# Unit 0 of a local-attention and channel-mix kernel split in two units of whole words, with a new plan

## The chip, the cores and the metric

The kernel runs on one core of one Trainium2 chip. The metric is device time in microseconds of one execution; the kernel before takes 609.59 (median of 3 runs, 609.19 to 614.19). The engines are PE (TensorE: matmuls into PSUM; PEld are its weight loads), DVE (VectorE), ACT (ScalarE), POOL (GpSimd) and SP (SyncE, which here only issues DMAs).

## What is computed

Attention with a window of 64 over 8 batches, 8 heads, 576 positions and 64 columns per head; its output is the input x of a channel mix with a gate (512 model columns, 1024 hidden columns). Cut from the reference:

```python
scores = np.where((rel >= 0) & (rel < 64), scale * np.matmul(q, k.transpose(0, 1, 3, 2)), -1e9)
scores = scores - np.max(scores, axis=-1, keepdims=True)
attn = np.exp(scores)
attn = attn / (np.sum(attn, axis=-1, keepdims=True) + 1e-09)
x = np.matmul(attn, v)                       # heads side by side: 512 columns
...
xk = mu_k * x + (1.0 - mu_k) * x_prev        # x_prev: x moved by one position
xr = mu_r * x + (1.0 - mu_r) * x_prev
k = np.maximum(xk @ w_k, 0.0)
v = k * k @ w_v
r = 1.0 / (1.0 + np.exp(-(xr @ w_r)))
return (r * v).astype(np.float32)
```

q, k, v and the mu are 32-bit; w_k (512x1024), w_v (1024x512) and w_r (512x512) come as 64-bit floats and are made into 32-bit ones on the chip.

## The kernel before

**Attention.** Positions go in blocks of 64, two blocks (128 tokens) are a group, 36 groups in all. A group's tiles by the names in the profile: scores s on PE from k and q; DVE folds the two key blocks into one (`s<-own,s`, `s<-s,hide`), takes the maximum (`most`); ACT makes exponentials and their sums (`pr`, in a "lean" group one row of heads at a time with the sum taken along; in the others DVE subtracts and sums); DVE scales (`rs`, `pr<-pr,rs`); for the first ten groups PE transposes (t), later ones go through DVE and two DMAs; DVE masks (`pt`, two steps); PE multiplies with v (x), and ACT copies x into the unit's buffer `xu`.

**Channel mix.** Tokens go in units of 256 (18 of them, `UNITS`). Each unit has mixing (xk and xr), k products (`m<-xk,w`, then relu `kf` and square `ks`), r products (`m<-xr,w`, then `th`, `r` and the gate's share `r<-th,r`), v products (`m<-ks,w`), and the gated result (`r<-m,r`), which SP stores. A product is made for two column blocks of 128 at a time into one PSUM bank.

**Weights.** Twenty chunks of 128x512 (four of w_r, eight of w_k, eight of w_v). Each is loaded by a DMA, then decoded from 64 to 32 bits: one ACT step (`wt<-w`), two short DVE steps on `wt`, and two long ones (`wt<-w,wt` and, last, `w<-w,wt`, which puts the 32-bit word in place). From unit 1 on, products don't use the word but two parts of it, a high and a low one in a one-pass type (fp32r), three one-pass records per product. The parts are made by `split`: ACT copies the high part (CAST `w<-w`), DVE subtracts for the low one (`w<-w,w`); for chunk 0 (`PE_LOW`) PE makes the low part with two matmuls of 512 columns (`m<-w,ident`, `m<-w,minus`) and ACT copies it. The decoded words must stay until their chunk is split.

**Unit 0** uses the whole words, before they are split: mixing on PE with diagonal matrices (`mixer`, made on ACT), then r, k and v products of 256 columns as whole-word matmuls. Each of these is two records in the trace. It needs x of groups 0 and 1, and each product its decoded chunk. Unit 1 mixes with ACT and DVE (`e<-xu,mu` on ACT, blend `e<-xu,muk,e` and `e<-xu,mur,e` on DVE, then high and low parts xk, xr), later units with DVE alone for the blend.

**What sets the order.** Every step is a Piece with an engine, a key, an assumed cost and what it needs and holds. `play()` walks a clock of its own over all pieces, on each engine takes the ready one with the lowest key, and the instructions are emitted in that order; each engine then runs them strictly in it. The keys of the plan are the tables at the top: `BEGIN` (attention bursts), `DECODE` and `SPLIT` (chunks), `MIX_*`, `SOFT`, `MIXER`, the set `LEAN`, and `ORDER` for the first loads on SP's queue. All instructions carry one line number in the profile, since a wrapper records them.

## Time and profile before

| | us |
|---|---|
| median of 3 runs | 609.59 (609.19 to 614.19) |
| profiled execution, its own time | 611.41 |
| its span, first to last instruction | 609.5 |

Busy time of each engine over the span, from the page's first part (share, and count of instructions):

```profile
PE 585.8 (96%) x7131; PEld 572.5 (94%) x7131; DVE 437.8 (72%) x974; ACT 334.2 (55%) x741; POOL 9.4 (2%) x39
```

The second part cuts the span in 40 slices of 15.2 us; a digit is the busy share in tenths:

```profile
PE   2689999999999999999999999999999999999997
DVE  5889999486959586868686778768777668686321
```

PE is full from the fourth slice to the last but one; DVE is full only in slices four to six. What differs from slice to slice lies in the first five.

### The profile page before, as it was taken

What the parts mean: (1) busy time and instruction counts of PE and PEld (TensorE: products, weight loads), DVE (VectorE), ACT (ScalarE), POOL (GpSimd) and SP (SyncE); (2) the same over time, 40 slices, a digit from 0 to 9 for tenths busy, and PEclk for the clock granted to TensorE, in tenths of its full rate; (3) what the DMA queues carried; (4) which work ended last, traced back from release to release, by engine and by line L of the source; (5) the groups of instructions that cost most, each with busy time, mean ns of one, the idle gap of its engine ahead of it and who ended that gap; (6) DMA issues with size and microseconds to landing.
All of it is one profiled execution on the core that took longest, in us unless ns stands there. A gap on an engine that the chain in (4) does not pass through costs nothing.

```text
span 609.5 us, 17060 instructions
## 1 busy us (share of the span) xinstructions
PE 585.8 (96%) x7131; PEld 572.5 (94%) x7131; DVE 437.8 (72%) x974; ACT 334.2 (55%) x741; POOL 9.4 (2%) x39
## 2 busy tenths in 40 slices
PE   2689999999999999999999999999999999999997
PEld 1578899999999999999999999999999999999997
DVE  5889999486959586868686778768777668686321
ACT  5758878381927182727363646354645455454442
POOL 5000000000000000000000000000000000000000
PEclk9999999999999999999999999999999999999999
DMA  9877232314433242425242525242524252121011
GB/s 276 282 238 250 62 97 61 99 51 122 131 93 117 74 146 79 139 74 163 80 130 70 157 71 148 70 140 88 143 84 139 75 153 72 55 70 36 2 35 36
DMA packets 98269, 67.18 MB, mean 110 GB/s; under 512 B 15504, under 2 KB 92304, under 8 KB 98192
## 3 DMA queue, kind: packets, MB, share of 16 engines
q1 hardware_dynamic: 97904, 66.09, 35.9%
q8 instruction: 56, 0.92, 0.6%
q14 instruction: 21, 0.17, 0.1%
q10 hardware_dynamic: 288, 0.00, 0.0%
HBM read 49.81 MB, written 16.25 MB: 108 GB/s over the span
## 4 chain that ended last, share of the span: by engine, by line
PE 89%; DMA 6%; DVE 2%; ACT 1%; SPq 1%; issue 0%; ACTq 0%
PE m L94 79%; PE s L94 5%; PE x L94 5%; DMA w<-w_k 2%; DMA w<-w_r 1%; DMA w<-w_v 1%; DVE wt L94 1%; SPq L94 1%; DMA k<-kT 1%; PE t L94 1%; DVE w L94 0%; ACT pr L94 0%; ACT e L94 0%; DVE r L94 0%; ACT xu L94 0%
## 5 line engine op out<-in xcount | busy, mean ns | idle before, releaser
L94 PE MATMUL m<-xk,w 128*128 128x256 f32 x1696 | 225.1, 282 | 0.3 <-issue 0.3
L94 PE MATMUL m<-ks,w 128*128 128x256 f32 x1696 | 222.6, 281 | 0.8 <-issue 0.5
L94 PEld LDWEIGHTS m<-xk,w 128*128 128x128 f32 x1696 | 208.2, 188 | 2.7 <-issue 0.4
L94 PEld LDWEIGHTS m<-ks,w 128*128 128x128 f32 x1696 | 207.4, 188 | 3.3 <-issue 1.1
L94 PE MATMUL m<-xr,w 128*128 128x256 f32 x848 | 122.6, 280 | 0.0
L94 PEld LDWEIGHTS m<-xr,w 128*128 128x128 f32 x848 | 108.9, 188 | 0.8 <-ACT xr L94 0.2
L94 ACT ACTIVATE kf<-m 128x512 f32<-128x512 f32 x72 | 42.9, 597 | 88.7 <-PE m L94 87.7
L94 DVE TENSOR_TENSOR ks<-kf,ks 128x512 fp32r<-128x512 f32 x68 | 46.0, 678 | 57.6 <-ACT ks L94 57.5
L94 ACT COPY xu<-x 128x512 f32<-128x512 f32 (+3 forms) x28 | 19.4, 712 | 119.0 <-PE x L94 118.9
L94 DVE SCALAR_TENSOR_TENSOR r<-m,r 128x512 f32<-128x512 f32 (+1 forms) x37 | 24.9, 676 | 65.8 <-PE m L94 65.8
L94 PE MATMUL s<-k,q 64*64 64x128 f32 (+1 forms) x1152 | 37.5, 279 | 9.5 <-DMA q<-qT 9.5
L94 PEld LDWEIGHTS s<-k,q 64*64 64x64 f32 x1152 | 31.9, 140 | 13.1 <-issue 7.8
L94 ACT ACTIVATE kf<-kf 128x512 f32<-128x512 f32 x68 | 43.3, 636 | 1.6
L94 ACT CAST ks<-kf 128x512 fp32r<-128x512 f32 x68 | 42.5, 625 | 1.5
L94 PE MATMUL x<-pt,v 64*64 64x64 f32 (+1 forms) x1664 | 35.9, 237 | 0.1
L94 PEld LDWEIGHTS x<-pt,v 64*64 64x64 f32 x1664 | 34.7, 136 | 1.0 <-issue 0.8
L94 DVE TENSOR_TENSOR pt<-pr,sides 128x512 f32<-128x512 f32 x52 | 34.1, 684 | 0.7 <-DMA pr<-far 0.7
L94 DVE COPY_PREDICATED s<-own,s 128x256 f32<-128x256 uint32 (+1 forms) x72 | 25.5, 395 | 11.6 <-PE s L94 10.7
L94 DVE SCALAR_TENSOR_TENSOR r<-th,r 128x512 f32<-128x512 f32 x36 | 24.6, 682 | 11.6 <-ACT r L94 11.5
L94 DVE SCALAR_TENSOR_TENSOR e<-d,mur,xu 128x256 f32<-128x256 f32 (+3 forms) x88 | 31.1, 405 | 0.0
L94 DVE SCALAR_TENSOR_TENSOR e<-d,muk,xu 128x256 f32<-128x256 f32 (+3 forms) x88 | 30.6, 403 | 0.0
L94 ACT ACTIVATE th<-m 128x512 f32<-128x512 f32 x36 | 21.7, 603 | 13.7 <-PE m L94 13.6
(65 smaller groups left out, 517.4 us busy)
## 6 DMA issues: line engine op xcount, KB each, us to landing
k<-kT SPq DMA_DIRECT2D x28, 384.0 KB, 4.7
q<-qT SPq DMA_DIRECT2D x32, 256.0 KB, 4.1
v<-v SPq DMA_DIRECT2D x128, 64.0 KB, 3.3
far<-tr SPq DMA_DIRECT2D x26, 256.0 KB, 2.0
pr<-far SPq DMA_DIRECT2D x104, 64.0 KB, 1.9
outT<-r SPq DMA_DIRECT2D x23, 256.0 KB, 2.2
w<-w_k SPq DMA_DIRECT2D x8, 512.0 KB, 6.1
w<-w_v SPq DMA_DIRECT2D x8, 512.0 KB, 6.3
```

The costliest lines, as they stand in the source:

```text
L94: return lambda *args, **kw: tc.keep_in_program_order(op(*args, **kw))
```

## The change

`UNITS` becomes (2, 2) and then 17 units of 4: the first 256 tokens are two units of 128, each made of one group, and both use whole words (`EXACT = 2`). Unit 2 takes the place of unit 1 in how it mixes. The products of both are put in with keys from a table: r and k of unit 0, r and k of unit 1, and only then v of both. The results ks of two pairs of column blocks share one buffer, there are four r buffers for three. All the plan's tables are new; `PE_LOW` is empty, so DVE makes every low part; `LEAN` loses groups 6 and 11.

```diff
-UNITS = (4,) * 18
+UNITS = (2, 2) + (4,) * 17
-R_BUFS = 3
+R_BUFS = 4
...
-LEAN = {0, 1, 2, 3, 4, 6, 7, 8, 10, 11}
-PE_LOW = {0}
+LEAN = {0, 1, 2, 3, 4, 7, 8, 10}
+PE_LOW = set()
+EXACT = 2
+FRONT = (("r", 0, 0), ("k", 0, 8), ("r", 1, 24), ("k", 1, 32), ("v", 0, 48), ("v", 1, 64))
...
-ORDER = (*"w k0 q0 w k1 q1 w k2 w v1 w w w v0 q2 v3 w w q5 w w v4 w k3 w k4 w k5 q3 v2 w v5 w w w w w".split(),
-         *"q4".split())
+ORDER = (*"q0 k0 w k1 q1 w w k2 w v0 w q4 q2 v1 w w w v3 w v2 q3 w w w k5 v4 w w w k3 v5 w q5 w w w".split(),
+         *"k4 w".split())
...
-        if u == 0:
+        if u < EXACT:
             (_, _, _, x0), = parts(u)
...
-            state, scratch, result = [], Hold("tmp"), Hold("ks")
+            state, scratch = [], Hold("tmp")
+            result = k2[-1][1] if first and i % 2 else Hold("ks")
...
-                    state.append(act.tile([P, 2, n], F32, name="ks0", tag="ks", bufs=KS_BUFS))
+                    if i % 2 == 0:
+                        both.append(act.tile([P, 2, 2, n], F32, name="ks0", tag="ks", bufs=KS_BUFS))
+                    state.append(both[-1][:, i % 2])
...
+        early[u] = xk, xr, gate, k2
+        if u < EXACT - 1:
+            continue
+        for what, e, key in FRONT:
+            xk, xr, gate, k2 = early[e]
+            if what == "r":
+                r_units(key, *xr, gate, n, True)
+            elif what == "k":
+                k_units(key, *xk, k2, n, True)
+            else:
+                v_units(key, e, k2, gate, n, True)
```

What moves is shown at three places, before and after. In these rows a name's number stays where it tells tiles apart.

PE, start of the program, before: scores of group 2, values of group 1 (the four x rows), then mixing of unit 0 (three of its four pieces) and the first r product.

```order
L94 MATMUL s<-k,q 64x128 x16
L94 MATMUL x<-pt,v 64x128 x4
L94 MATMUL x<-pt,v 64x64 x8
L94 MATMUL x<-pt,v 64x128 x4
L94 MATMUL x<-pt,v 64x64 x8
L94 MATMUL m<-xu,mixer 128x256 x12
L94 MATMUL t<-ident,pr 128x4x32 x4
L94 MATMUL m<-xr_448,w_118 128x256
```

The same place after; the transposition t in the first row is group 1's, and group 0's values stand ahead of it:

```order
L96 MATMUL t<-ident,pr 128x4x32 x4
L96 MATMUL s<-k,q 64x128 x16
L96 MATMUL m<-xu,mixer 128x128 x8
L96 MATMUL x<-pt,v 64x128 x4
L96 MATMUL x<-pt,v 64x64 x8
L96 MATMUL x<-pt,v 64x128 x4
L96 MATMUL x<-pt,v 64x64 x8
L96 MATMUL m<-xu,mixer 128x128 x8
L96 MATMUL m<-xr_437,w_126 128x128
```

Mixing of unit 0 begins ahead of group 1's values instead of behind them.

PE, v products of unit 0 before: the rows from the low part for chunk 0 to the first product of the second pair of columns (`ks_683,w_474` is its first chunk). w_538 is the chunk that DVE decodes last.

```order
L94 MATMUL m<-w_118,ident 128x512
L94 MATMUL m<-w_705,minus 128x512
L94 MATMUL m<-ks_687,w_516 128x256
L94 MATMUL m<-ks_687,w_531 128x256
L94 MATMUL m<-ks_720,w_538 128x256 x2
L94 MATMUL m<-ks_720,w_543 128x256 x2
L94 MATMUL m<-ks_842,w_556 128x256 x2
L94 MATMUL m<-ks_842,w_605 128x256
L94 MATMUL t<-ident,pr 128x4x32 x4
L94 MATMUL m<-ks_683,w_474 128x256
```

After: `ks_604` and `ks_684` are unit 0's, `ks_803` and `ks_830` unit 1's, w_525 is the first chunk of w_v, and w_610 the one that DVE decodes last.

```order
L96 MATMUL m<-ks_830,w_590 128x128
L96 MATMUL m<-ks_830,w_599 128x128
L96 MATMUL m<-ks_684,w_610 128x128 x2
L96 MATMUL m<-ks_604,w_525 128x128 x2
L96 MATMUL m<-ks_604,w_557 128x128 x2
L96 MATMUL m<-ks_604,w_564 128x128 x2
L96 MATMUL m<-ks_604,w_577 128x128 x2
L96 MATMUL m<-ks_684,w_583 128x128 x2
L96 MATMUL m<-ks_684,w_590 128x128 x2
L96 MATMUL m<-ks_684,w_599 128x128 x2
L96 MATMUL m<-ks_684,w_610 128x128 x2
L96 MATMUL m<-ks_830,w_610 128x128 x2
```

The chunk decoded last now closes the first pair of columns of unit 0, and the second pairs of both units stand behind it; before, the fifth chunk of the first pair was the one decoded last, and 24 products stood from it on.

DVE, the end of decoding before (group 4's first steps, unit 1's blends e, the last step of w_538):

```order
L94 SCALAR_TENSOR_TENSOR w_543<-w_543,wt 128x512
L94 TENSOR_REDUCE most<-s 128x4 x2
L94 TENSOR_TENSOR w_709<-w_128,w_709 128x512
L94 SCALAR_TENSOR_TENSOR wt<-w_538,wt 128x512
L94 SCALAR_TENSOR_TENSOR e<-xu,muk,e 128x256 x2
L94 SCALAR_TENSOR_TENSOR w_538<-w_538,wt 128x512
L94 SCALAR_TENSOR_TENSOR e<-xu,muk,e 128x256 x2
```

And after (unit 2's blends, the last step of w_610):

```order
L96 TENSOR_TENSOR s<-s,hide 128x2x64
L96 SCALAR_TENSOR_TENSOR wt<-w_610,wt 128x512
L96 TENSOR_REDUCE most<-s 128x4 x2
L96 SCALAR_TENSOR_TENSOR e<-xu,muk,e 128x256 x4
L96 SCALAR_TENSOR_TENSOR e<-xu,mur,e 128x256 x4
L96 SCALAR_TENSOR_TENSOR w_610<-w_610,wt 128x512
L96 TENSOR_TENSOR w_824<-w_126,w_824 128x512
```

All eight blends stand ahead of the last decode step instead of two, and the first split of a chunk behind it. On SP's queue q and k of group 0 now lead, and the chunks of w_k are issued ahead of the v that crosses two batches (eight DMAs).

More of the change, by code (lines that the diff above doesn't have):

```diff
@@ L43 @@
 USTEPS = 40
[L44 to L57 removed]
+BEGIN = (-219.0, -153.0, -33.5, -13.0, 19.5, 25.0, 56.5, 67.0, 99.5, 120.5, 130.5, 154.5, 211.5, 216.5, 218.5,
+    231.5, 264.5, 268.5, 276.0, 329.0, 337.5, 341.0, 393.0, 415.0, 446.5, 455.0, 466.0, 513.5, 526.5, 546.5,
+    551.0, 563.0, 602.0, 609.0, 620.0, 627.0, 695.0)
+DECODE = (318.0, -62.5, -227.0, 24.0, 94.5, -374.5, -288.0, 11.0, 5.0, -70.0, 202.0, 362.5, -58.0, 381.0,
+    -84.5, 120.0, -310.0, -167.0, 12.5, 192.5)
+MIX_0 = (-210.5, -67.0, -379.5, 166.0)
+MIX_1 = (154.0, -358.5)
+MIX_N = (365.0, 83.5)
+SPLIT = (313.75, 318.25, 49.5, 394.5, -175.25, 79.5, 239.5, 145.75, -311.0, -373.0, 196.5, 173.5, 122.5,
+    -255.5, 153.5, 86.0, 227.0, 426.5, 233.0, 101.0)
+SOFT = (-196.5, -253.0, -250.0, 61.5, 287.0, 357.5)
+LEAN = {0, 1, 2, 3, 4, 7, 8, 10}
+PE_LOW = set()
+EXACT = 2
+FRONT = (("r", 0, 0), ("k", 0, 8), ("r", 1, 24), ("k", 1, 32), ("v", 0, 48), ("v", 1, 64))
+MIXER = (64.5, 212.5)
 SPARE = {512: 2}
@@ L658, in mix @@
         pk = None
-        if u >= 2:
+        if u > EXACT:
             scratch = Hold("tmp")
@@ L684, in blend @@
             def blend(e=e, mu=mu, xs=xs, hold=hold):
-                if u >= 2:
+                if u > EXACT:
                     e.append(pair(tmp.tile([P, 512], F32, name="e", tag="tmp", bufs=TB), n))
@@ L701, in low @@
                 dve.tensor_sub(xs[0][:, 1, cs, :n], e[0], xs[0][:, 0, cs, :n].bitcast(F32))
-            if u >= 2:
+            if u > EXACT:
                 p = Piece("DVE", key, 2 * over(n) + 130, blend, [pk], [own_], [held["x", u], scratch], port=True)
@@ L778, in k_units @@
     def k_units(key, xk, hold, made, k2, n, first):
+        both = []
         for i in range(NF // 2):
@@ L803, in k_units @@
             p = Piece("ACT", key, acts(2 * n), relu, [p], [scratch], [bank])
-            p = Piece("ACT", key, acts(2 * n) + 20, square, [p], [result] if first else [], [scratch])
+            p = Piece("ACT", key, acts(2 * n) + 20, square, [p], [result] if first and i % 2 == 0 else [],
+                      [scratch] + ([result] if first and i % 2 else []))
             if first:
@@ L877, in attn_rwkv_kernel @@
             prefetch(t, [("q", g + 2), ("k", g + 2)] + [("v", g)] * (t > LATE))
+    early = {}
     for u, nb in enumerate(UNITS):
@@ L883, in attn_rwkv_kernel @@
         xk, xr = ([], Hold("xk"), []), ([], Hold("xr"), [])
-        if u == 0:
-            keys = MIX_0
-        elif u == 1:
+        if u < EXACT:
+            keys = MIX_0[2 * u:2 * u + 2]
+        elif u == EXACT:
             keys = MIX_1
@@ L891, in attn_rwkv_kernel @@
             mix(u, i, keys[i], xk, xr)
-        if u == 0:
-            r_units(base, *xr, gate, n, True)
-            k_units(base + 8, *xk, k2, n, True)
-        else:
+        if u >= EXACT:
             k_units(base, *xk, k2, n, False)
             r_units(base + 16, *xr, gate, n, False)
-        v_units(base + 24, u, k2, gate, n, u == 0)
-        if u == 0:
-            for i in range(len(chunks)):
-                split(i)
+            v_units(base + 24, u, k2, gate, n, False)
+            continue
+        early[u] = xk, xr, gate, k2
+        if u < EXACT - 1:
+            continue
+        for what, e, key in FRONT:
[6 more added lines that the diff above has]
+                v_units(key, e, k2, gate, n, True)
+        for i in range(len(chunks)):
+            split(i)
     for p in play():
```

16 lines of the change are left out of this document (2 added, 14 removed).

## The prediction

> **What bounds the kernel now.** I read the page's totals first, then the engines by stage, then the chain that ended last, and only then single rows of the start.
>
> ```profile
> span 609.5 us, 17060 instructions
> 0.00:27.04 27.04, 10.21 (x185) 8.29 (x185) 18.96 (x44) 17.70 (x65) 8.67 (x32) 1.00 0.88 270
> 27.04:34.55 7.51, 5.91 (x28) 4.94 (x29) 5.31 (x13) 5.64 (x24) 0.00 (x0) 1.00 0.65 221
> 34.55:68.03 33.48, 32.07 (x289) 27.48 (x287) 32.26 (x72) 24.06 (x69) 0.10 (x1) 1.00 0.74 237
> 68.03:81.30 13.27, 13.06 (x133) 11.38 (x133) 12.89 (x26) 10.43 (x25) 0.00 (x0) 1.00 0.06 20
> 81.30:606.34 525.04, 524.58 (x6500) 520.43 (x6500) 367.97 (x824) 276.37 (x563) 0.63 (x6) 1.00 0.32 95
> 606.34:609.50 3.16, 0.00 (x0) 0.00 (x0) 0.42 (x1) 0.00 (x0) 0.00 (x0) 0.90 0.37 124
> ```
>
> After the stretch and its length the columns are busy time of PE, PE's weight loads, DVE, ACT and POOL, then granted clock, DMA share and GB/s. From 81.30, where the first product of split words starts, to 606.34, PE idles 0.46 us of 525.04; the tail is 3.16 us. The products of split words and the attention groups behind that point are the same after the change. So the time is the moment of that first split product (I call it the anchor, 81.30 now) plus 528.2, and whatever the change gives must show as an earlier anchor. Ahead of it PE idles 20 us, 18.4 of them before 34.55, while DVE is 96% busy from 34.55 to 68.03. Here is what leads to the anchor, from the chain of waits:
>
> ```profile
> 70.21 1.57 PE m L94 x6
> 71.78 0.44 PE t L94 x4
> 72.22 7.35 PE m L94 x34
> 79.57 1.03 PE s L94 x32
> 80.60 0.70 PE x L94 x48
> 81.30 8.04 PE m L94 x69
> ```
>
> And the rows at about 62 to 68 us (engine, operation, tile written <- tiles read):
>
> ```profile
> 61.80 0.63 PE L94 MATMUL x<-pt,v 64*64 64x128 f32 x24
> 66.56 0.87 DVE L94 SCALAR_TENSOR_TENSOR e<-xu,muk,e 128x256 f32<-128x256 f32 x2
> 67.35 0.68 DVE L94 SCALAR_TENSOR_TENSOR w<-w,wt 128x512 uint32<-128x512 uint32 x1
> 68.13 1.97 PE L94 MATMUL m<-ks,w 128*128 128x256 f32 x8 [0.48 <-issue]
> ```
>
> The row at 67.35 is the last decode step of the last weight chunk (w_538); it ends at 68.03, and PE, which had come to exactly that chunk in its order, starts 0.1 us later. From there to the anchor PE does 24 whole-word products (48 records: 8, 6 and 34), one transposition and one group's scores and values, 13.3 us without a real gap. So the anchor is the end of decoding on DVE, T = 68.03, plus 13.3. The idle PE of the first 27 us is not by itself on this path: DVE is.
>
> **The change part by part.** First the price of a whole-word record of 128 columns, which the trace does not have. A record of 256 columns costs 7.35 / 34 = 0.216 us. Streaming half the columns would be 0.108. The other bound comes from rows with 128x128 weights loaded for each record:
>
> ```profile
> 34.09 0.63 PE L94 MATMUL t<-ident,pr 128*128 128x128 f32 x4 [1.60 <-ACT xr L94]
> 34.55 0.60 PE L94 MATMUL m<-xr,w 128*128 128x256 f32 x2
> L94 PEld LDWEIGHTS m<-xr,w 128*128 128x128 f32 x848 | 108.9, 188 | 0.8 <-ACT xr L94 0.2
> ```
>
> Four transposing records of 128 columns go from 34.09 to 34.55, 0.115 each, and the one-pass records from 81.30 take 8.04 / 69 = 0.117, each with its own load. So 0.108 to 0.117; I take 0.115, the row with the same column count. Twice as many records at 0.115 make 0.230 per pair instead of 0.216: the 192 whole-word records of unit 0 (mixing, r, k, v) cost 41.5, the 384 after it 44.2, 2.7 us more PE work. All but the part behind T lies in PE time that waits for DVE anyway.
>
> A rule speaks against this. The Trainium skill, "TensorE: Matmul & The Clock Gate", LDWEIGHTS, gives a load about 1/1.2 ns per column, an estimate of 107 ns for 128 columns, and in The mechanism says that a load overlaps a running matmul only when the row group differs. By its first part load and stream would be equal at 128 columns and the sum stays; by the second nothing would hide, which is the third rival below. The trace does not agree with the second: 0.115 to 0.117 per record with a 128x128 load in each leaves no room for both in turn.
>
> Start of PE. These are the rows that lead to the first mixing:
>
> ```profile
> 6.81 1.55 PE L94 MATMUL s<-k,q 64*64 64x64 f32 x32 [6.81 <-DMA q<-qT]
> 8.46 0.30 DVE L94 TENSOR_TENSOR s<-s,hide 128x128 f32<-128x128 f32 x1 [0.71 <-PE s L94]
> 9.63 0.39 ACT L94 ACTIVATE mixer<-ident,mur 128x128 f32<-128x128 f32 x1
> ...
> 11.97 0.20 ACT L94 ACTIVATE most<-most 128x8 f32<-128x8 f32 x1
> 16.02 1.09 PE L94 MATMUL t<-ident,pr 128*128 128x128 f32 x4 [2.98 <-DVE pr L94]
> 21.37 1.56 PE L94 MATMUL x<-pt,v 64*64 64x128 f32 x32
> 27.04 5.45 PE L94 MATMUL m<-xu,mixer 128*128 128x256 f32 x24 [0.97 <-ACT xu L94]
> ```
>
> Group 0's q and k are now issued ahead of the first weight chunk, which moves its scores from 6.81 to about 5.4; ACT no longer makes eight mixers (9.63 to 11.97, 2.3) ahead of its exponentials, so these begin at about 9.4; its values need not follow group 1's transposition, and unit 0 needs only this group. Its transposition comes at about 13.4 and its values at 16.5; ACT then still makes group 1's exponentials and the mixers before it copies x, so the first mixing moves from 27.04 to about 21. The r products wait for group 2's exponentials on ACT too, and move from 34.55 to about 28.4, 6.2 us earlier. None of it counts unless T moves.
>
> T. DVE's waits until then, with the row kinds that change:
>
> ```profile
> DVE wt L94 <- ACT wt L94: 8.2, 3, 5.4
> DVE s L94 <- PE s L94: 1.1, 2, 0.7
> DVE rs L94 <- ACT rs L94: 1.0, 2, 0.5
> DVE pt L94 <- PE x L94: 0.6, 1, 0.6
> L94 DVE SCALAR_TENSOR_TENSOR r<-m,r 128x256 f32<-128x256 f32 x2 | 0.8, 425 | 2.6 <-PE m L94 2.6
> L94 DVE SCALAR_TENSOR_TENSOR r<-th,r 128x512 f32<-128x512 f32 x2 | 1.4, 690 | 0.0
> ```
>
> The waits add to 10.9 (5.4 of them at the start), so DVE works 57.1 us up to T. After the change the order has the same 20 decodes and the same four and a half groups ahead of the last decode step (now of w_610), but all eight blends e of unit 2 where two stood (six more at 0.87 / 2 = 0.43: +2.6), four r steps of 256 columns for two of 512 (4 x 0.425 - 2 x 0.69 = +0.3), and no split of a chunk (-0.7, as the 0.68 of a step of this size). DVE works 59.3. Its first instruction now waits for group 0's scores: 5.4 + 1.65 (8.46 - 6.81) = 7.1 instead of 5.4. Of the other 5.5 us of waiting, the 2.8 for ACT's first decode step come from late chunks; w_k's chunks are now issued ahead of the large v, so I let them go. But DVE gets a wait that it had not: the unit 0 step r<-th stands ahead of the last decode step of w_208, the first chunk that k needs, and it waits for ACT, where copies of unit 1's mixing stand ahead of its inputs. Between 0 and the 5.5 that all these waits cost now I put 2.2, and 1.3 for the rest. T = 7.1 + 59.3 + 3.5 = 69.9, 1.9 later; the ends are 66.4 (no wait but the first) and 71.9.
>
> From T to the anchor. After the change PE's order has w_610 as the last chunk of unit 0's first pair of columns, so all second pairs stand behind it: 36 products, 72 records at 0.115 = 8.3, the transposition 0.44, scores and values 1.73 (81.30 - 79.57): 10.5 instead of 13.3. At 0.108 it is 10.0. The part of the low half that PE made for one chunk (two records of 512 columns) is gone from PE and DVE does it behind T, where it has until w_r is needed.
>
> ACT's work on units 0 and 1 doubles in count:
>
> ```profile
> L94 ACT COPY xu<-x 128x256 f32<-128x256 f32 x5 | 1.8, 375 | 11.3 <-PE x L94 11.3
> L94 ACT ACTIVATE th<-m 128x512 f32<-128x512 f32 x36 | 21.7, 603 | 13.7 <-PE m L94 13.6
> ```
>
> Forty steps of 256 columns at 0.375 for twenty of 512 at about 0.6 are 3.0 us more; ACT is 72% busy from 34.55 to T (24.06 of 33.48), so this is hidden but for the 2.2 above. A fourth r buffer and two k results in one ks buffer add no instruction.
>
> Sum: anchor 69.9 + 10.5 = 80.4, 0.9 earlier than 81.30. Behind it I cost everything at nothing: the fourth split that k's first columns need is the nineteenth DVE row behind T, fourteen of about 0.6 and five of 0.2 to 0.4, some 10 us, just inside the 10.5; two groups more go through the longer DVE softmax, but DVE is 70% busy there (367.97 of 525.04) and waits for PE. If that cover is gone, the next thing late is w_k's second half. The profiled execution took 611.41 for its span of 609.5; the median of the three runs is 609.59, so its own 610.5 answers to 608.7 for the median.
>
> **The rivals.**
>
> The head start carries through (faster). If PE set the end, 6.2 us would stay: 603.4 (609.59 - 6.2). For it: PE idles 16.8 us to 27.04. Against it: DVE's 96% until T; T would have to be 64.6, below the 66.4 that DVE's work alone takes. Between 603.4 and 606 only if my DVE sum is too high by several steps.
>
> DVE's last decode waits for PE (slower). The eight blends stand ahead of w_610's last step and need the values of group 3, which PE does behind all k products of unit 1. Now that values row ends at 62.43 and T follows 5.6 later. After the change PE has, from 28.4, 230 records (26.5), and 4.9 of attention, and about 2.5 of waiting for w_208: 62.3, so T = 67.9 by this path, 2 us before DVE's own 69.9. It decides once that values row ends after 64.3, and costs a microsecond for each one. If PE keeps none of the head start (r products at 34.55), T = 74.1 and the time 612.9. For it: the first transposition takes 1.09 where the one at 34.09 takes 0.63, so early PE work runs at half speed although the granted clock reads 1.00, and it now holds the mixing too. The Trainium skill, in the same page under What's actually happening, says that the array's clock is throttled until some 3.4 us of activity; the two transposition rows agree.
>
> Nothing of the load hides (slower by much). Each record costs 0.188 of load more: 230 records up to group 3's values and 72 behind T make 57 us, less 2 of slack: about 663. Against it stands the 0.117 of one-pass records.
>
> **How the numbers follow.** My forecast (606 to 610.5) has 0.62, the head start (602 to 606) 0.11, the late blends (610.5 to 614) 0.23, exposed loads 0.01, and 0.03 is left for what I don't see. The likeliest is 608.7. The range 604.5 to 612.5 cuts half of the first rival and a part of the second, and holds DVE's ends (605.2 and 610.7). One per cent, about what a measurement of this kernel can tell from no change, is 6.1 us: faster than 603.5 has 0.07, slower than 615.7 0.05, the rest 0.88.
>
> **What would show it.** Right: the last decode step on DVE ends at 68 to 71, PE's first split product at 79 to 81.5, whole-word records of 128 columns at about 0.115, first mixing at about 21, PE idle behind the anchor still under 1 us. Wrong: records of 128 columns at 0.2 or more; an idle DVE in front of the blends for xu (the late blends); a last decode step well before 66; or idle PE behind the anchor, in front of k or r products, for a split that DVE had not made.

## The result, and the profile after

The changed kernel takes 619.58 us (median of 5 runs, 617.82 to 620.97), the kernel before beside it 611.83 (5 runs, 609.19 to 614.19): a ratio of 1.0128, with a 95% interval of 1.0083 to 1.0173. It is slower, and 7 us above the predicted range; the kernel before beside it lies 2.2 us above the 609.59 of three runs from which the prediction started. In all runs beside the experiments the kernel before lay at medians of 611.1 to 612.2, and the changed kernel, run once more, gave 619.34, 1.0126 (1.0083 to 1.0170).

| us | before | after | predicted |
|---|---|---|---|
| span of the profiled execution | 609.5 | 619.1 | |
| first k product on PE | 42.85 | 40.88 | |
| end of decoding, T | 68.03 | 73.47 | 69.9 |
| from T to the anchor | 13.2 | 10.92 | 10.5 |
| anchor (first split product) | 81.23 | 84.39 | 80.4 |
| anchor to the end of the last product | 525.10 | 531.37 | as before |
| tail | 3.17 | 3.34 | as before |

So 3.2 us are lost ahead of the anchor and 6.3 behind it. (The table takes the anchor from the row in which the split product is the first of its run, 81.23, where the prediction took it from the chain, 81.30.)

First the engines by stage after the change, cut at the first r product, the first k product, T, the anchor and the end of the last product (columns as in the prediction: PE, its weight loads, DVE, ACT, POOL, granted clock, DMA share, GB/s):

```profile
0.00:29.37 29.37, 14.10 (x217) 11.91 (x217) 20.16 (x48) 20.42 (x85) 7.35 (x32) 1.00 0.88 266
29.37:40.88 11.51, 8.05 (x69) 7.88 (x69) 8.76 (x19) 7.12 (x20) 0.11 (x1) 0.95 0.79 223
40.88:73.47 32.59, 32.59 (x380) 32.09 (x380) 29.48 (x68) 22.94 (x78) 0.00 (x0) 0.91 0.58 200
73.47:84.39 10.92, 10.92 (x157) 10.68 (x157) 10.51 (x21) 7.67 (x19) 0.00 (x0) 1.00 0.14 38
84.39:615.76 531.37, 530.38 (x6502) 526.01 (x6501) 372.63 (x833) 274.63 (x533) 0.64 (x6) 1.00 0.31 93
615.76:619.10 3.34, 0.01 (x1) 0.00 (x0) 0.42 (x1) 0.00 (x0) 0.00 (x0) 1.00 0.35 118
```

Two lines matter. From the first k product to T PE is busy for all of 32.59 us, at a mean clock of 0.91; DVE is 90% busy there (29.48). Before, PE had waits in that stretch and DVE had next to none. And behind the anchor the stretch is 6.3 us longer, though PE idles only 1.0 us in it (531.37 - 530.38) and makes the same products.

PE's rows of the start, in the timeline after the change (start, length, then the idle time before a row and who ended it):

```profile
29.37 1.21 PE L96 MATMUL m<-xr,w 128*128 128x128 f32 x8 [1.53 <-ACT xr L96]
...
40.88 7.44 PE L96 MATMUL m<-xk,w 128*128 128x128 f32 x40 [3.46 <-ACT th L96]
48.16 0.63 PE L96 MATMUL m<-xr,w 128*128 128x128 f32 x4
...
57.59 4.87 PE L96 MATMUL m<-xk,w 128*128 128x128 f32 x40
62.30 0.60 PE L96 MATMUL t<-ident,pr 128*128 128x128 f32 x4
...
66.38 1.08 PE L96 MATMUL x<-pt,v 64*64 64x128 f32 x48
67.39 11.58 PE L96 MATMUL m<-ks,w 128*128 128x128 f32 x94
```

PE waits 3.46 us for the first k product. The row names ACT's th, but what came last is DVE's last decode step of the first w_k chunk (w_208), which ran from 40.10 to 40.78; in the second profile, too, the product starts 0.10 us behind the end of that step (40.77 and 40.67). The first 40 records then take 7.28 us to the start of the next row; at 57.59 forty records of the same kind take 4.71. From 40.88 on no row has an idle time shown (the timeline leaves out those under 0.15), up to the anchor. DVE's rows up to T, with its last wait:

```profile
62.94 0.69 DVE L96 TENSOR_TENSOR pt<-t,sides 128x512 f32<-128x512 f32 x1 [0.33 <-PE t L96]
...
69.62 1.66 DVE L96 SCALAR_TENSOR_TENSOR e<-xu,muk,e 128x256 f32<-128x256 f32 x4
71.20 1.67 DVE L96 SCALAR_TENSOR_TENSOR e<-xu,mur,e 128x256 f32<-128x256 f32 x4
72.78 0.69 DVE L96 SCALAR_TENSOR_TENSOR w<-w,wt 128x512 uint32<-128x512 uint32 x1
```

The last decode step stands directly behind the eight blends, and these need the values of group 3, which PE ended at 67.39 (the start of the row behind them). T follows 6.07 us later; in the second profile of the changed kernel 6.07 as well (66.33 and 72.40). The row at 62.94 shows how close it is: DVE waits there 0.33 us for group 3's transposition, which PE does just ahead of that group's values (the row at 62.30), and from there to T it works without a wait. So PE holds DVE, but only by some 0.3 us. DVE's waits up to T (total, times, longest):

```profile
DVE wt L96 <- ACT wt L96: 7.1, 4, 2.7
DVE s L96 <- PE s L96: 6.7, 2, 6.2
DVE rs L96 <- ACT rs L96: 0.6, 1, 0.6
DVE pt L96 <- PE t L96: 0.3, 1, 0.3
```

They add to 14.7, so DVE works 58.8 us up to T. Why the first 40 records are slow is read from the granted clock, the third column from the end in these rows of one microsecond each:

```profile
39.00:40.00 1.00, 0.00 (x0) 0.00 (x0) 1.00 (x3) 1.00 (x4) 0.00 (x0) 0.81 0.13 39
40.00:41.00 1.00, 0.12 (x1) 0.15 (x1) 1.00 (x3) 1.00 (x4) 0.00 (x0) 0.50 0.07 19
45.00:46.00 1.00, 1.00 (x7) 1.00 (x6) 1.00 (x2) 0.00 (x0) 0.00 (x0) 0.50 0.98 384
46.00:47.00 1.00, 1.00 (x9) 1.00 (x9) 0.06 (x1) 0.00 (x0) 0.00 (x0) 0.77 1.07 375
```

The clock falls to half inside PE's wait, at about 39.6 (0.81 is 0.38 of a microsecond at half speed), and comes back at about 46.5.

Behind the anchor the difference is in the rate of the products. Rows of three one-pass records just behind the score burst at 280 us, in the changed kernel:

```profile
287.95 0.52 PE L96 MATMUL m<-xr,w 128*128 128x256 f32 x3
288.30 0.52 PE L96 MATMUL m<-xk,w 128*128 128x256 f32 x3
288.65 0.52 PE L96 MATMUL m<-xr,w 128*128 128x256 f32 x3
```

and the same rows in an experiment with the same order from there on (unit 1's r products ahead, without ten clamps, below):

```profile
286.53 0.50 PE L96 MATMUL m<-xk,w 128*128 128x256 f32 x3
286.87 0.50 PE L96 MATMUL m<-xr,w 128*128 128x256 f32 x3
287.21 0.50 PE L96 MATMUL m<-xk,w 128*128 128x256 f32 x3
```

Starts lie 0.353 us apart (mean of several) in the first and 0.340 in the second: one has 3.7% less throughput, with PE busy throughout and the clock at 1.00 in both. A rate holds from one attention burst or stall to the next. I call stretches of over 5 us at 0.353 that end past 160 us long stretches (earlier every profile has shorter ones, of 3 to 8 us each, before the change too). Before has none; this execution has them from 285 to 311, 348 to 404 and 472 to 531, 133 us in all without the attention between them.

### The profile page after: what moved, and what is told of

Read it like the earlier page. It is cut to its first block, busy times and chain, and to the rows that moved or that the text cites. A ratio compares the mean times of both kernels' runs of the same rounds, so it can differ in the third digit from the quotient of the medians.

```text
span 619.1 us, 17412 instructions
## 1 busy us (share of the span) xinstructions
PE 596.0 (96%) x7320; PEld 588.6 (95%) x7320; DVE 442.0 (71%) x985; ACT 332.8 (54%) x729; POOL 8.1 (1%) x39
## 4 chain that ended last, share of the span: by engine, by line
PE 91%; DMA 4%; DVE 2%; SPq 1%; ACT 1%; issue 1%; ACTq 0%; DVEq 0%
PE m L96 82%; PE s L96 5%; PE x L96 4%; DMA w<-w_k 2%; SPq L96 1%; DMA q<-qT 1%; DVE s L96 1%; PE t L96 1%; DVE most L96 1%; ACT kf L96 0%; DVE pr L96 0%; ACT ks L96 0%; ACT th L96 0%; DVE r L96 0%; ACT r L96 0%
## 5 line engine op out<-in xcount | busy, mean ns | idle before, releaser
L96 PE MATMUL m<-xk,w 128*128 128x256 f32 (+1 forms) x1760 | 229.2, 281 | 4.3 <-ACT th L96 3.5
L96 PE MATMUL m<-ks,w 128*128 128x256 f32 (+1 forms) x1760 | 222.2, 278 | 0.2 <-DVE r L96 0.2
L96 PEld LDWEIGHTS m<-xk,w 128*128 128x128 f32 x1760 | 215.0, 191 | 6.0 <-ACT th L96 3.6
L96 PEld LDWEIGHTS m<-ks,w 128*128 128x128 f32 x1760 | 211.1, 189 | 0.8 <-DVE r L96 0.4
L96 PE MATMUL m<-xr,w 128*128 128x256 f32 (+1 forms) x880 | 120.4, 278 | 1.5 <-ACT xr L96 1.5
L96 ACT ACTIVATE kf<-m 128x512 f32<-128x512 f32 (+1 forms) x76 | 43.5, 574 | 138.7 <-PE m L96 138.4
L96 DVE SCALAR_TENSOR_TENSOR r<-m,r 128x512 f32<-128x512 f32 (+1 forms) x39 | 25.3, 648 | 46.5 <-PE m L96 46.5
L96 PE MATMUL s<-k,q 64*64 64x128 f32 (+1 forms) x1152 | 37.4, 279 | 8.9 <-DMA k<-kT 4.6
L96 DVE SCALAR_TENSOR_TENSOR r<-th,r 128x512 f32<-128x512 f32 (+1 forms) x38 | 24.9, 655 | 10.2 <-ACT r L96 10.0
L96 ACT ACTIVATE th<-m 128x512 f32<-128x512 f32 (+1 forms) x38 | 21.9, 576 | 17.4 <-PE m L96 17.2
L96 ACT CAST xr<-e 128x512 fp32r<-128x512 f32 x34 | 21.2, 622 | 18.6 <-DVE e L96 18.6
```

The source lines that it names most:

```text
L96: return lambda *args, **kw: tc.keep_in_program_order(op(*args, **kw))
```

## The experiments

All 20 profiles in one table; each row's edit follows below. "k" is the first k product on PE.

| profile | k | k to anchor | anchor | anchor to last product | long stretches, us in all |
|---|---|---|---|---|---|
| before | 42.85 | 38.38 | 81.23 | 525.10 | 0 |
| before, again (r_before) | 42.46 | 38.06 | 80.52 | 525.35 | 0 |
| b_clamp | 45.21 | 37.06 | 82.27 | 525.03 | 0 |
| b_rbuf | 43.52 | 37.16 | 80.68 | 524.67 | 0 |
| b_fill16 | 48.26 | 37.06 | 85.32 | 524.75 | 0 |
| b_t2 | 47.05 | 37.07 | 84.12 | 526.00 | 0 |
| b_t2_clamp | 45.55 | 37.06 | 82.61 | 525.85 | 0 |
| after | 40.88 | 43.51 | 84.39 | 531.37 | 133 |
| after, again (r_after) | 40.77 | 42.55 | 83.32 | 529.45 | 81 |
| e_first | 38.10 | 45.32 | 83.42 | 527.42 | 26 |
| e_warm | 41.43 | 41.34 | 82.77 | 534.82 | 190 |
| e_r1 | 47.37 | 39.71 | 87.08 | 526.79 | 0 |
| e_clamp | 41.01 | 41.16 | 82.17 | 533.43 | 185 |
| e_r1c | 45.21 | 37.52 | 82.73 | 526.61 | 0 |
| e_less | 40.00 | 41.20 | 81.20 | 533.02 | 139 |
| e_nostall | 42.86 | 41.26 | 84.12 | 529.43 | 82 |
| e_nostall2 | 40.85 | 42.29 | 83.14 | 526.69 | 0 |
| e_tail | 42.18 | 41.27 | 83.45 | 526.82 | 0 |
| e_warm_tail | 41.71 | 41.39 | 83.10 | 530.62 | 81 |
| e_clamp_tail | 40.95 | 42.54 | 83.49 | 531.89 | 138 |

### Ahead of the anchor

**Twice more without an edit.** The changed kernel and the kernel before, for what one execution differs from the next.

> The changed kernel once more, unaltered. Two things are asked: does the stretch from the first split product to the last matmul (531 us in its first profile, 525 in that of the kernel before, for the same products) come out at 531 again, and do the stretches with 0.353 us per three one-pass records (against 0.340) lie between the same attention bursts (285 to 311, 348 to 404, 470 to 531 us)? Theory P (the order of instructions decides the rate): yes to both, within 1 us. Rival C (chance of an execution): the stretch anywhere from 525 to 535, the slow stretches elsewhere. Start as before: clock 0.5 from 40.9 to 46.5, first split product at 84.4 within 0.5.

> The kernel before once more, for its trace. Theory P: 525 us from the first split product (81.3) to the last matmul, rate 0.340 but for 132 to 150 us. Rival C: another length, up to 530.

619.34 and 610.95. The anchor came at 83.32 and 80.52.

**The first w_k chunk earlier (e_first).** Three DVE steps change places: the last decode step of w_208 goes right behind the step ahead of it, the two r<-th of unit 0 behind the last step of w_301.

```diff
+    behind(whole[4], uppers[4])
+    last = whole[7]
+    for _, _, p in early[0][2]:
+        behind(p, last)
+        last = p
```

> The changed kernel with three DVE steps moved and nothing else: the last decode step of the first w_k chunk right behind the step before it, and unit 0's two r<-th steps behind the last decode step of w_301. Theory A (the late start is the 3.5 us in which PE waits for that chunk, and the half clock that follows): PE starts k at 37.3, waits under 2 us in one piece, keeps clock 1.0; the last decode step on DVE ends at 69 to 71 instead of 73.5, the first split product stands at 80 to 82 instead of 84.4, and the time falls by 3 to 4 us. Rival B (DVE's work alone sets the end of decoding, PE's wait is hidden): 73 and 84 again, no gain.

619.44, 1.0141 (1.0099 to 1.0183). PE begins k at 38.10 instead of 40.88, then waits 1.17 and 1.14 us for the next chunks and still loses clock (0.50 from 42.7 to 46.1). T 72.49, anchor 83.42, against 84.39 and 83.32 in the two profiles without an edit: nothing gained. Theory A's forecasts missed, but the edit did not give it its condition: the wait moved in between the k products (2.3 us in two pieces) and did not go away.

**PE kept busy (e_warm).** Sixteen idle products fill its wait for the first k product.

```diff
+                        if whole_ and w is wk_s and not filled:
+                            filled.append(1)
+                            for _ in range(FILL):
+                                pe.matmul(made_[0][:, 0], word_of(0)[:, :P], early[0][1][0][0][:, 0], start=True, stop=True)
```

> The changed kernel with 16 whole-word matmuls of 128 columns more on PE (32 records, 3.8 us) ahead of the first k product, into the bank that this product then overwrites. PE has work in the time in which it waits, and the wait itself stays. Theory A with the clock as the larger part: no half clock behind 40.9, the first split product about 2.9 us earlier (81.5). If the wait is what counts and the clock little: 84 again. Rival B: 84 again, and the end of decoding at 73.5.

620.46, 1.0147 (1.0104 to 1.0190). The clock stays at 1.00, and from k to the anchor PE takes 41.34 instead of 42.55 and 43.51. That prices the half clock at 1.2 and 2.2 us. But k begins 0.6 later, so the anchor, 82.77, is only 0.6 to 1.6 better, less than the expected 81.5, and T is 71.84, far from the 69.9 that DVE's work alone was to give.

**Less work for DVE (e_clamp).** The first decode step (the clamp of the exponent's range) is left out for the last ten chunks, 3.4 us of DVE; ACT's first step of w_525 goes ahead of the first relu.

```diff
+    for n in range(10, 20):
+        clamps[n].fn = lambda: None
+    k0 = pieces[slice(*spans["k", 0])]
+    ahead(next(p for p in lines["ACT"] if p in k0), signs[12])
```

> The changed kernel, with VectorE's first decode step (the clamp, 0.34 us) left out for the last ten chunks, 3.4 us of VectorE's work between 42 and 67 us, and ACT's first step of the first w_v chunk ahead of the first relu. Left out is the clamp of the exponent's range for these ten chunks. Theory I: VectorE ends decoding at 68.5 to 70.5, but TensorE, full since 42.5, gets to the last chunk at 72 as before: first split product 82.3 to 83.8, 12.5 to 14 us behind the end of decoding instead of 10.9. Theory D: 10.9 us behind the end of decoding, 79.5 to 81.4. Theory T: 82.3 to 83.8, as I. Time 616 to 620 by I and T, 613 to 617 by D.

620.21, 1.0137 (1.0099 to 1.0175). Timeline of PE:

```profile
41.01 5.09 PE L96 MATMUL m<-xk,w 128*128 128x128 f32 x40 [3.27 <-ACT th L96]
...
64.16 1.08 PE L96 MATMUL x<-pt,v 64*64 64x128 f32 x48
65.17 11.58 PE L96 MATMUL m<-ks,w 128*128 128x128 f32 x94
```

In this execution the wait of 3.27 us cost no clock. The values row ends at 65.17 and T comes at 71.25, again 6.07 later: with 3.4 us less to do DVE ends no earlier than PE lets it, and waits 0.57 us for the transposition instead of 0.33. The anchor is 82.17, and PE's 41.16 from k to it are the 41.3 of the kernel with the filler. DVE's load (theory D) does not set it. The expected T of 68.5 to 70.5 was wrong, since I had let go what the last decode step stands behind.

**Less work for PE (e_r1, e_r1c, e_less).** In the first, unit 1's r products go ahead of unit 0's k, where PE waits. In the second this goes with the ten clamps left out.

```diff
+    for p in r1:
+        p.needs = [q for q in p.needs if q not in k0]
+    for e in ("PE", "ACT"):
+        ahead(next(p for p in lines[e] if p in k0), *[p for p in lines[e] if p in r1])
+    ahead(lines["DVE"][lines["DVE"].index(whole[11]) + 1], *[p for p in lines["DVE"] if p in r1])
```

> The changed kernel with unit 1's r products (32 records of 128 columns, 3.8 us) ahead of unit 0's k products on TensorE, their four ACT steps each with them, and their two steps r<-th,r on VectorE behind the last decode step of the last w_k chunk. They fill TensorE's wait for the first w_k chunk (2.8 to 3.5 us in two executions of the changed kernel) and take 3.8 us out of the work behind it. Theory I (interlocked: from 42.5 us to the end of decoding TensorE and VectorE are both full and reach the last w_v chunk together; in the execution looked at TensorE got to it at 72.2 and VectorE had it at 72.4): relief of TensorE alone buys nothing, since it then waits for VectorE: end of decoding 71.5 to 73.5, first split product 82.3 to 84, TensorE idle 2 to 4 us between 50 and 73 us. Theory T (TensorE's own work behind its wait sets the first split product): 79.5 to 80.5. Theory D (VectorE's decoding alone sets it): 82.5 to 84, as I. Behind the first split product nothing was altered: 527 to 535 as in the four executions so far, time 616 to 620 by I and D, 613 to 617 by T.

> Both edits together: unit 1's r products ahead of unit 0's k, and the clamp of the last ten chunks left out. Theory I: only now both engines have less to do, and the first split product comes at 79.5 to 81.5, 2 to 4 us earlier, with the end of decoding at 68.5 to 70.5 and 10.9 us between. Theory T: as with the first edit alone, 79.5 to 80.5. Theory D: as with the second alone. Under I neither edit alone moves it by more than 1 us. Time 613 to 617, since behind the first split product nothing is altered (527 to 535).

619.24, 1.0119 (1.0084 to 1.0154), and 617.37, 1.0104 (1.0056 to 1.0151). PE in the first:

```profile
41.23 6.34 PE L96 MATMUL m<-xr,w 128*128 128x128 f32 x28 [3.13 <-ACT xr L96]
47.37 7.74 PE L96 MATMUL m<-xk,w 128*128 128x128 f32 x64
...
64.97 0.63 PE L96 MATMUL t<-ident,pr 128*128 128x128 f32 x4 [2.31 <-DVE pr L96]
```

All three theories missed the anchor of 87.08. Unit 1's r products were no filler: their xr comes from ACT as late as the first k chunk from DVE, so PE waits 3.13 in the new place and k begins 6.5 us later. What the pair does show is the work behind k: 39.71 less the wait of 2.31 is 37.4, and 37.52 with less for DVE, 3.8 below 41.3. That is unit 1's r (32 records of 0.1177, the row at 57.59 being 4.71 to the next row's start for 40). The pair was no test of the time that theory I forecast, since neither edit freed what I meant to free. But it shows its mechanism: once PE has 3.8 us less to do behind k, DVE, which has its full work and waits 3.01 us for ACT's first decode step, is the later one, and PE waits 2.31 us for its pr; with the ten clamps left out it waits only 0.16.

So in the third PE has less to do at the place where it is full: without ten clamps, and three quarters of unit 1's r products left out (24 records, 2.8 us).

```diff
+                        if thin_ and c:
+                            return
...
+            thin[0] = what == "r" and e == 1
```

> The kernel without ten clamps (VectorE relieved), with TensorE relieved too in the place where it is full: of unit 1's 16 r products only the first chunk's four are made, 24 records of 128 columns or 2.8 us less. Left out are the products of three of w_r's four chunks for unit 1. Theory T (in the changed kernel TensorE's own work since its first k product sets the first split product: 41.2 us at full clock in the execution without the ten clamps, and the last decode step follows it, since it stands behind blends that wait for group 3's values on TensorE): the first split product comes 1.2 to 2.8 us earlier than there (82.2), at 79.4 to 81.0, less than 2.8 only if the transposition of group 2 then waits for VectorE; end of decoding still 10.9 us ahead of it. Theory D (VectorE's decoding sets it): 82 as there. Behind it 527 to 535.

618.40, 1.0103 (1.0050 to 1.0157).

```profile
40.00 7.62 PE L96 MATMUL m<-xk,w 128*128 128x128 f32 x40 [3.32 <-ACT th L96]
...
63.03 1.08 PE L96 MATMUL x<-pt,v 64*64 64x128 f32 x48
64.04 11.74 PE L96 MATMUL m<-ks,w 128*128 128x128 f32 x94
```

The anchor is 81.20, 0.2 outside what theory T expected, since this execution fell into the half clock (40 records in 7.62). Against the changed kernel's own profile, with the same half clock, k to the anchor is 41.20 for 43.51, 2.3 of the 2.8 us taken out; against the execution without ten clamps and with the full clock, 2.5 once the 40 records' 2.5 us (7.62 - 5.09) are taken off. Theory T holds here, where DVE has 3.4 us less to do: less work for PE from the first k product on moves the anchor. T is 6.24 behind the values row and no longer 6.07, and DVE has no wait for PE's transposition left: now DVE is the later one. Less work for PE alone at this place is not tested by any run; by the 0.33 us of slack that DVE has in the changed kernel I estimate that it would gain little more than that. So the two engines are nearly interlocked, as theory I had it, with PE the later one by that little.

**The same clamps left out before the change (b_clamp).**

```diff
+    begun = play()
+    for n in range(10, 20):
+        clamps[n].fn = lambda: None
```

> The kernel before without the clamp of the last ten chunks, 3.4 us less on VectorE, which is the edit that moved the changed kernel's first split product by 1.2 us (no more than its TensorE clock explains). Left out is the clamp of the exponent's range for these ten chunks. If VectorE is the bound before the change, as TensorE's waits there (0.99 and 0.48 us between 55 and 70 us) let it seem, and TensorE only after it: end of decoding 64.5 to 66, first split product 78 to 79.5, time 608 to 610.5. If TensorE was already the bound before: first split product 80 to 81, time 610 to 612.

612.71, 1.0014 (0.9979 to 1.0048): no gain. Neither expectation held, since here k began at 45.21, 2.4 us later than in the first profile (mixing began late, behind ACT's xu). But from there PE took 37.06 to the anchor, with one wait of 0.77, and four of the seven profiles with the old front show 37.06 or 37.07. In the two where k began earliest, at 42.46 and 42.85, PE waited 0.80 and 0.99 us for DVE's pr and took 38.06 and 38.38. So before the change too PE was nearly full from k on, and DVE held it up by about a microsecond.

### Behind the anchor

**The old order behind the new front (e_tail).** All keys from group 10 on are those of the old plan: `BEGIN` from its eleventh number on plus 40 (one unit), `SOFT`, and

```diff
-MIX_N = (365.0, 83.5)
+MIX_N = (310.5, -406.0)
...
-LEAN = {0, 1, 2, 3, 4, 7, 8, 10}
+LEAN = {0, 1, 2, 3, 4, 7, 8, 10, 11}
```

> The changed kernel with the old plan's numbers for everything from group 10 on (start keys of the bursts moved by one unit, the mixing keys, the softmax keys and the set of lean groups); the first 90 us are in the changed kernel's order. Theory P (the new plan's order behind the first split product costs time: scores of two groups that find TensorE's banks taken, and longer stretches at 0.353 us for three records instead of 0.340): from the first split product to the last product 525 to 526 as before the change, no stretch of 0.353 past 150 us, time 612.5 to 615. Theory C (the rate is chance of the execution, and the order does not decide): 527 to 535 as in the four executions of the changed order, time 616 to 621. The first split product stays at 82.5 to 84.5 by both.

618.05, 1.0115 (1.0052 to 1.0177). The profile has no long stretch, 526.82 behind the anchor, but the runs spread from 615.27 to 623.83, and the median is the changed kernel's within the uncertainty. The order behind the anchor is at most part of it.

**The new order behind the old front (b_t2), and a fourth r buffer alone (b_rbuf).** The first has the new plan's `BEGIN` less 40 from its thirteenth number on, its `SOFT`, and the first of these diffs; the second has only the other.

```diff
-MIX_N = (310.5, -406.0)
+MIX_N = (365.0, 83.5)
...
-LEAN = {0, 1, 2, 3, 4, 6, 7, 8, 10, 11}
+LEAN = {0, 1, 2, 3, 4, 6, 7, 8, 10}
```

```diff
-                          pair(tmp.tile([P, 2 * TU], F32, name="r", bufs=R_BUFS), n)]
+                          pair(tmp.tile([P, 2 * TU], F32, name="r", bufs=R_BUFS + 1), n)]
```

> The kernel before with the new plan's numbers from group 12 on (bursts moved back by one unit, mixing, softmax, lean groups); its first 90 us are in the order of before. Theory P (the new order behind the first split product costs time): from there to the last product 526.5 to 527, with stretches at 0.353 us for three records begun at the bursts near 280, 345 and 475 us in half of the executions; time 612 to 619, median 614 or more, 3 us above the kernel before. Theory C (which rate follows a burst is chance whatever the order): 525 to 531 and the kernel before's own spread, 609 to 615, median within 1 us of it.

> The kernel before with one more buffer for r (four, as the change has), and nothing else: the same order of instructions, but every tile allocated behind it lies elsewhere in memory. Theory L (the rate of one-pass records depends on where the tiles lie, which the change moves too): stretches at 0.353 us past 150 us, time 612 to 619. Theory C: the spread of the kernel before, 609 to 615, median within 1 us of it.

614.31, 1.0047 (1.0021 to 1.0073), and 613.17, 1.0010 (0.9983 to 1.0037). The new order costs 526.0 behind the anchor, 0.8 more than the mean of the two before (its stalls over 0.3 us, 0.35 and 0.43, are little more than in the old order, which has one of 0.43 in one of the two profiles and none in the other), and no long stretch; the median is 2.1 us above that of before beside it, between the two theories, and this profile's k comes late (47.05). The r buffer changes nothing.

**Two more looks at the new front with the old order, and one at the old front with the new order.** The edits are those above put together: the filler with the old order, the ten clamps left out with the old order, and the ten clamps left out before the change with the new order.

> The changed kernel with the filler products on TensorE that kept its clock at 1.00 (they gave a first split product at 82.8) and with the old plan's numbers from group 10 on. If the slow rate needs both the new front and the new order behind it: no slow stretch past 170 us, 526 to 527 from the first split product to the last product, first split product 82 to 83.5, median 614 to 616.5. If it comes of the front alone, or of chance: slow stretches here too, 527 to 534, median 617 to 620.

> The changed kernel without the clamp of the last ten chunks (which is left out) and with the old plan's numbers from group 10 on; with the new numbers it had slow stretches from 286 to 336 and from 474 to the end, and 620.2. If the slow rate needs both: no slow stretch past 170 us, 526 to 527 behind the first split product, which comes at 81.5 to 84, median 613.5 to 617. If it comes of the front alone, or of chance: 527 to 534, median 617 to 621.

> The kernel before without the clamp of its last ten chunks (which is left out) and with the new plan's numbers from group 12 on. If the slow rate needs both: none past 230 us, 525.5 to 526.5 behind the first split product, median 612 to 615. If the new order alone lets it set in: slow stretches at 280, 345 or 475, 527 to 533, median 615 to 619. The first split product lies at 80 to 84 as in the five profiles of the old front, with 37.1 us from the first k product to it where TensorE does not wait.

618.89, 1.0126 (1.0097 to 1.0156), with long stretches from 250 to 276 and 347 to 405; 620.07, 1.0137 (1.0106 to 1.0168), with them from 344 to 501; and 612.81, 1.0021 (1.0002 to 1.0039), with none. So the long stretches don't need the new order. In these 20 profiles they come with the new front alone.

**The stalls (e_nostall, e_nostall2).** In the changed kernel PE stalls 0.49 us behind the burst at 280 us, for DVE's pr. DVE's low step of ks, for which DVE sat waiting 4.5 us, goes behind the folds of the scores.

```diff
+        if i + 1 < len(row) and row[i + 1].fn.__name__ == "pack" and i > row.index(whole[19]):
+            while row[i + 1].fn.__name__ == "pack":
+                row[i], row[i + 1] = row[i + 1], row[i]
+                i += 1
```

> The changed kernel, with one VectorE step moved at four score bursts of two groups behind the first split product (VectorE's low step of ks, for which it sat waiting 4.5 us for ACT, goes behind the folds of the scores instead of ahead of them), all else in its order. The stall of TensorE there (0.49 us, VectorE's pr frees the PSUM banks late) goes: 0.5 to 1 us less. Theory S (such a stall is what lets the slower rate of 0.353 us for three records set in, as it did right behind it in five of eight profiles): no slow stretch begins at 283 to 290, behind the first split product 525.5 to 528, median 615 to 617.5. Theory C (it sets in by chance at any burst): slow stretches as often as in the changed kernel, 526 to 535 behind, median 618 to 620.

> The changed kernel, with VectorE's low step of ks behind the folds of the scores instead of ahead of them at every score burst behind the end of decoding, the one at 280 us among them, where TensorE stalled for 0.49 us in all nine profiles of this order. The stall at 283 to 284.5 goes (a stall that the trace puts down to no other engine, near 345, need not). Theory S (a stall lets the slower rate set in): no slow stretch begins at 283 to 290, median 615 to 617. Theory C (it sets in at any burst): the burst at 280 is followed by either rate, slow stretches past 160 us as in 9 of 12 profiles with this front, median 616.5 to 619.5.

617.04, 1.0094 (1.0065 to 1.0123), and 617.99, 1.0103 (1.0064 to 1.0142). The diff is the second's; the first chose by the key of the fold in place of its row, missed the burst in question and moved four others. The second moved it, and the stall stayed: 0.53, as DVE has now the wait for PE's scores (4.57) instead of the one for ks, and pr comes where it came. So neither took the stall away, and that is left open. But the second says something else:

```profile
283.48 3.32 PE L96 MATMUL m<-xk,w 128*128 128x256 f32 x27 [0.53 <-DVE pr L96]
286.64 0.50 PE L96 MATMUL m<-xr,w 128*128 128x256 f32 x3
```

the same stall, followed by the quick rate, as in e_r1, e_r1c and e_less. The stall doesn't decide which rate follows.

**More records on PE in the old front (b_fill16).** Sixteen idle products of 128 columns ahead of the first r product.

```diff
+                    if whole_ and w is wr_s and not filled:
+                        filled.append(1)
+                        for _ in range(16):
+                            pe.matmul(made_[0][:, 0, :P], word_of(0)[:, :P], x(c, 0)[:, :P], start=True, stop=True)
```

> The kernel before with 16 whole-word products of 128 columns (32 records, 3.8 us) put on TensorE ahead of its first r product, and nothing else. The first split product comes 1 to 4 us later, at 82 to 86. If more work and instructions on TensorE in the front are what lets the slower rate set in behind it: slow stretches past 160 us, more than 526 us from the first split product to the last product, and a time that is 3 us or more above what the later first split product gives. If not: none past 160 us, 524.7 to 525.4, as in the four profiles of before's order, median 612 to 616.

615.56, 1.0070 (1.0048 to 1.0091). The anchor is at 85.32, and behind it 524.75 without a long stretch: the time is what the later anchor gives. More work on PE ahead is not what lets the slower rate set in.

## Why the prediction was wrong

Of the time that the prediction had for the span (80.4 + 528.2 = 608.6, measured 619.1), 4.0 us are missed ahead of the anchor and 6.3 behind it. So two steps failed: the engine that sets T, and the nothing that was put behind the anchor, which is the larger. The steps in their order:

**The record of 128 columns: right.** 0.1177 us (4.71 / 40 from the row at 57.59 to the next) for the 0.115 taken; a 128x128 load in each is hidden. In the Trainium skill, "TensorE: Matmul & The Clock Gate", The mechanism, one sentence has a load overlap only when the row group differs; these records contradict that sentence, as the prediction had it. (The same section also has loads pulled ahead into a background weight buffer, which would fit them.)

**From T to the anchor: right.** 10.92 for 10.5, in all 13 profiles of the new front 10.92 or 10.93.

**DVE's work up to T: right in size, and not the step that counts.** 58.8 for 59.3. The prediction set T = first instruction + work + waits = 69.9, with DVE as the engine that sets it. This is the first step that failed. PE sets T: the last decode step stands behind steps of DVE that need group 3's transposition and values, and it came 6.07 or 6.08 us behind those values in 12 of the 13 profiles with the new front, the one where DVE had 3.4 us less to do among them. Taking work from DVE alone moved T and the anchor by no more than the clock and the start of k explain; taking it from PE as well moved the anchor. The sign that the prediction had named for this, an idle DVE in front of the blends, is not there in the profile after, since DVE is only 0.3 us ahead of PE.

That was the prediction's second rival, the late blends, with the right rule (it decides once the values row ends after 64.3, and costs a microsecond for each one) and the wrong sum. It put the end of the values row at 62.3; it was 67.39. The 5.1 us, term by term from the rows of the profile after: the r products began at 29.37 for 28.4 (1.0); PE waited 3.46 for the first k product and not 2.5 (1.0); the first 40 k records took 7.28 to the next row's start and not 4.71 (2.6; some 2.2 of it is the half clock, since the same records took 4.93 to 5.10 in the five profiles in which the clock read 1.00 there); and 230 records at 0.1177 for 0.115 (0.6). 1.0 + 1.0 + 2.6 + 0.6 = 5.2. By its own rule that is 3.1 us on T, and T came 3.6 late; the other 0.5 is the 6.07 from the values row to T, for the 5.6 that the rival took from before. The half clock is the largest, and the prediction had cited it for the first transposition and not carried it to the wait that it had itself put into the sum.

**PE's slack: wrong.** "All but the part behind T lies in PE time that waits for DVE anyway" was to hide the dearer records. From k to the anchor PE needs 41.3 us at full clock, waits under 0.15 us included. With the old front it took 37.06, a wait of 0.5 to 0.8 among them: 36.3 to 36.6 of work, 4.7 to 5.0 less. The terms are unit 1's r, which stood ahead of k before (3.8), 256 records of k and v for 128 (30.1 for 27.6, at 0.1177 and the prediction's 0.216), less 1.1 for the low part that PE no longer makes and 0.4 for two r records: 4.8. Against that k begins only 2.0 us earlier, at 40.88 for 42.85. From before's profile: 42.85 - 2.0 + 37.06 + 4.2 (41.3 - 37.06) + 2.2 of half clock = 84.3, and 84.39 was measured; the 1.3 us that PE took longer than 37.06 in that profile is what it had to give. The 6.2 us of head start were 5.2 at the first r product (29.37 for 34.55), and ended in the wait for w_208.

**The waits of DVE: mis-sized, with little effect.** 14.7 for 10.6, and with 3.4 us less work for DVE T still followed PE; 7.1 of them are for ACT's first decode steps, where the prediction had let the late chunks go.

**"Behind it I cost everything at nothing": wrong, and the larger miss.** PE idles 1.0 us there, as predicted, but that was not the right test: the products themselves took 0.353 instead of 0.340 for three in long stretches. Those of the first profile, 133 us, cost 4.9 (3.7% of 133); 531.37 less 4.9 is 526.5, and the four profiles of the new front without a long stretch have 526.6 to 526.8. So some 1.5 us is what the new front or order costs without them, against 525.1, of which two stalls of 0.3 to 0.6 each are seen. The rest is the slower rate. It showed in 9 of the 13 profiles with the new front, whether the old or the new order stood behind it, and in none of the 7 with the old front; if the front made no difference, all 7 would come out without one in about 1 of 235 draws. What of the front does it is open. Not by themselves: the order behind it, the fourth r buffer, more records on PE, the stall at 284. Not tried are the ks buffers that two results share, and with them where the later tiles lie. Nor does one front give one outcome: two profiles of the same kernel had 133 and 81 us of it.

For the 7.8 us between the medians that makes, as an estimate from the profiles, about 3 ahead of the anchor, 1.5 behind it in any case, and the rest the slower rate.

## What to carry to other kernels

Where two engines are both nearly full, write down the path of each to the end and follow the dependences of the step that is last, here the blends ahead of the last decode step: the wait that the profile shows before the change names the engine that was late by a little, and says nothing of how much slack the other has. Where both come to the end within a few tenths of a microsecond, less work for one of them buys no more than those. A wait put on PE can cost more than itself, since the clock can be halved for what follows (here up to 2.2 us behind a wait of 3.46). And "the same work behind this point" is only as good as its rate: compare the spacing of equal rows before and after, not only the idle time.

## What was not expected of the hardware

**The half clock comes in steps.** In the profiles with the new front the clock reads 0.50 for 6.83 us (39.63 to 46.45 in the first, by the trace's record of the clock), or 3.41 (42.13 to 45.54 in the second profile of the changed kernel), or not at all, as in the execution without ten clamps, after a wait of 3.27 us. The waits ahead of the half clock at the k products were 2.8 to 4.0 us long (in e_first two, of 1.17 and 1.14), so nearly equal waits cost 0 to 2.2 us. These records begin at 25.17 us before the change and at 22.56 after it; a clock of 1.00 in a row ahead of that, as in the prediction's first stretch, is no reading. The Trainium skill, "TensorE: Matmul & The Clock Gate", What's actually happening, has the clock set by a free-running window of activity of some 3.4 us; the trace agrees, with one or two such windows at half speed (3.41 and 6.83 us); that their place against the wait is chance fits, but no run shows it.

**One-pass products have two rates.** Three records start 0.340 or 0.353 us apart, at a granted clock of 1.00, and keep the rate until the next attention burst, transposition or stall. No row of the trace tells which will follow.
